# A decode kernel of two attention and two gated blocks: the 78 matmuls of constants on TensorE are left out

## The chip, the cores and the metric

The kernel runs on one core of one Trainium2 chip. The core has five engines with a queue of instructions each: TensorE (PE; its weight loads are listed apart as PEld), VectorE (DVE), ScalarE (ACT), GpSimd (POOL) and SyncE (SP), which here only issues DMAs. The metric is the device time in microseconds of one execution, as the median of several runs. A profile of one further execution gives the time of each instruction. A tile in SBUF lies on 128 partitions; matmuls write to PSUM, whose eight banks of 128 x 512 float32 are all in use here.

## The reference

Four tokens (a batch of 4, one position each) of width 512 go twice through the same attention block and the same gated block, with residuals and a layer norm without parameters ahead of each:

```python
def _A_ref(x, k_cache, v_cache, wq, wo):          # 32 query heads, 8 key/value heads, 4096 positions, head size 128
    q = (x @ wq).reshape(B, Sq, Hq, Dh).transpose(0, 2, 1, 3)
    k = jnp.repeat(k_cache, 4, axis=1)
    v = jnp.repeat(v_cache, 4, axis=1)
    p = softmax(einsum("bhqd,bhkd->bhqk", q, k) * Dh ** -0.5)
    o = einsum("bhqk,bhkd->bhqd", p, v)
    return o.transpose(0, 2, 1, 3).reshape(B, Sq, Hq * Dh) @ wo

def _B_ref(x, w_gate, w_up, w_down):              # width 1792 inside
    return (sigmoid(x @ w_gate) * (x @ w_up)) @ w_down

x = x + A(layernorm(x)); x = x + B(layernorm(x))
x = x + A(layernorm(x)); x = x + B(layernorm(x))
```

The caches are in bfloat16. One head of one batch element has 4096 x 128 keys and as many values, 1 MB each, and there are 32 of each kind. Both layers read the same caches.

## The kernel before

**Units and pairs.** A unit is one key/value head of one batch element in one layer: 64 units, taken as 32 pairs of heads in the order of the table `ORDER` (lines 22 to 55). Pairs of the second layer start as soon as their batch element has gone through its gated block, while other elements are still in the first layer.

**Memory.** SBUF has 12 slots of 1 MB (tile `slot`) and four more that hold `wq` at first (tile `wq`). Each slot holds the keys or the values of one unit. Some are kept for the second layer (`RET`), the others are loaded again. Loads are issued by SP in the order of the table `LOADS`; `pump` (line 523) issues as many as there are free slots. A load into a slot waits for the last reader of what was there before, and since SP's queue is in order, later loads wait behind it. `wo` and the gated block's weights have places of their own and come in the same order.

**Steps.** The main loop (line 1822) has 33 steps. In step k the scores and the softmax of pair k are worked out and the values of pair k-1 are applied. By tile and line: the keys are transposed in place by DVE in blocks of 32 x 32 (L1165, 2.2 us a slot); TensorE multiplies them with the queries into `S_ps` (`scores`, L1181); DVE takes the largest (`smax`, L1218 to L1224), TensorE spreads it (`spread_max`, L1241), DVE negates it (L1254), ACT takes the exponential and its sum (L1266), TensorE sums over partitions (`sums`, L1289) and DVE inverts (`inverse`, L1299); TensorE transposes the probabilities into `PT` (`ptrans`, L1311), ACT and DVE copy them to `pT` in 16 parts (L1345 and L1339); TensorE applies the values (`pv`, L1415) into `O_ps`, DVE divides (L1506), TensorE applies `wo` (L1567, or L1537 and L1550 in another form) and DVE adds to the token (L1588).

**Passes.** When all pairs of a batch element in the first layer are done, a pass of 23 pieces takes it through the layer norm, the gated block, the next layer norm and the queries of the second layer: sums for the norm on TensorE (L753, L815) with a reciprocal root by Newton steps on DVE (L781, L797), the up and gate projections (L974), the turning and the down projection (L1017, L1088, L1110), the query projection (L1035), its turning (L1066) and spreading (L879), and POOL's blocks (`q_blocks`, L904), on which the scores of that element's first pair wait. There are four passes, for four elements, at about 89 to 110, 143 to 163, 194 to 212 and 249 to 267 us.

**What sets the order.** Nothing is scheduled by a planner: each engine runs its instructions in the order in which the program records them. The order is written out in tables. Each step has nine places, 0 to 8, at which `do_steps(k, w)` is called (line 1666), and the tables say at which place of which step a piece of a pass, a turn of `wo`, or the first half of the next scores stands. Waits are worked out from what is read and written under names: `S.group` makes an instruction wait for the last writer and the readers since, and `prune` drops the waits that others already imply.

**The fills.** The table `FILL` (lines 150 to 155) says at which places constants are multiplied, and how many times. `fill(n)` (line 1197) records n matmuls on TensorE of the identity with the identity twice side by side, 128 x 256, into columns 256 to 511 of the bank `MS`, which nothing reads. It is recorded as reading the identity and as writing the names `MS` and `MSs`, so that the first matmul of a group waits for the readers of the maximum (DVE L1254) and of the sums (DVE L1299), and the next writer of either name waits for the group on TensorE itself. `do_steps` calls it ahead of the other pieces of its place; `tail_fill` calls it in the tail (key 33).

**The tail.** After the last pair's scores the values of that pair come in quarters (L1442). The last token's `wo` (L1776), its mean by weights summed earlier (L1798), the last gated block for all four tokens (L921, L2020), and the output follow.

Of the kernel before, what the change touches and what calls it, by code (L numbers as in the profile page):

```python
# [146 lines left out]
)  # L147


FILL = {  # L150
# [4 lines left out]
}  # L155


WSUM = (
# [153 lines left out]
def bass_interleave_layers__gqa_block_cached__glu_gated_glu__decode_kernel(  # L312
# [884 lines left out]
    def fill(n):  # L1197
        wide_id = ident_bf[:, :].unsqueeze(1).broadcast_to([P, 2, P])
        fns = [
            lambda e: e.matmul(  # L1200
                MS[:, 2 * P:4 * P].rearrange("p (i m) -> p i m", i=2), lhsT=ident_bf[:, :], rhs=wide_id,
                start=True, stop=True,
            )
        ] * n
        S.group("pe", fns, reads=IDENT, writes=["MS", "MSs"])

    def tail_fill(i):
        if FILL.get((NP + 1, i)):
            fill(FILL[NP + 1, i])

# [384 lines left out]
    def finish():  # L1595
        while undone:
            undone.pop()()
# [68 lines left out]
    def do_steps(g, w):  # L1666
        finish()
        if FILL.get((g, w)):
            fill(FILL[g, w])
        for m in wo_steps.pop((g, w), ()):  # L1670
# [459 lines left out]
```

## Time and profile before

| what | before |
|---|---|
| median of 3 runs | 303.74 us (303.08 to 305.57) |
| profiled execution, its own time | 306.06 us |
| its span, first to last instruction | 304.3 us |
| mean granted TensorE clock | 0.826 |
| TensorE, weight loads, DVE, ACT, POOL busy | 220.8, 154.8, 208.0, 133.0, 26.4 us |
| read from HBM | 115.61 MB, 380 GB/s over the span |
| matmuls of L1200 | 78, 14.9 us busy |

How to read the page and the views: PE's busy time counts a matmul from its start to its modelled end, so overlapping ones are counted once. A row of the windows view gives a stretch of the span, its length, the busy us of PE, PEld, DVE, ACT and POOL with the number of instructions, the granted clock (1.00 is full speed), the busy share of the 16 DMA engines, and GB/s. A row of the timeline gives the start, the length from the first to the last of a run of like instructions, the engine, the line and the operation with output and input, and in brackets the idle time ahead and what ended it. A row of the chain of waits gives start, length and what was on the chain. "issue" stands where the profile shows nothing that was waited for.

### The profile page before, as it was taken

Reading aid. Unit: us, or ns where it says so; the run is one execution under the profiler, and the core shown is the slowest. Engines: PE = TensorE matmul, PEld = TensorE weight load, DVE = VectorE, ACT = ScalarE, POOL = GpSimd, SP = SyncE. Lnnn points to the kernel's source line nnn. Section 1 sums busy time; section 2 is a strip of 40 time slices with the busy share of each in tenths; the row PEclk is TensorE's granted clock in tenths of the full one; section 3 lists DMA queues with packets and bytes.
Section 4 is the critical chain, followed back from the end, with each engine's and each line's share of the span. In section 5 each row is a group of like instructions: output and inputs, shape, how many; then the busy total and the mean of one; then the engine's idle time right before and its main releaser. Section 6 shows DMA issues by size and latency. Waiting matters only on the chain.

```text
span 304.3 us, 11550 instructions
## 1 busy us (share of the span) xinstructions
PE 220.8 (73%) x5030; PEld 154.8 (51%) x5030; DVE 208.0 (68%) x599; ACT 133.0 (44%) x531; POOL 26.4 (9%) x108
## 2 busy tenths in 40 slices
PE   0373577367479877977897876987686968958896
PEld 0331135234355565566565554754455855646695
DVE  4745899496567457986853987776796578648724
ACT  1031344152514334755371784635483552536510
POOL 0000000000000001100001100001000000012200
PEclk9995559695957967579997776999879799995979
DMA  7999999999999979999999999999999998999800
GB/s 284 419 403 415 412 415 421 415 418 419 417 421 402 386 277 424 426 418 418 403 420 421 415 422 415 423 415 423 416 423 415 378 417 323 392 400 423 328 11 3
DMA packets 19166, 116.35 MB, mean 382 GB/s; under 512 B 1960, under 2 KB 1964, under 8 KB 6444
## 3 DMA queue, kind: packets, MB, share of 16 engines
q1 hardware_dynamic: 19116, 115.62, 93.3%
q8 instruction: 39, 0.64, 0.8%
q14 instruction: 11, 0.09, 0.1%
HBM read 115.61 MB, written 0.00 MB: 380 GB/s over the span
## 4 chain that ended last, share of the span: by engine, by line
DMA 38%; PE 31%; DVE 19%; ACT 4%; issue 3%; SPq 3%; POOL 0%; DVEq 0%
DMA slot<-in_A_v_cache_dram 14%; DMA wo<-in_A_wo_dram 13%; DMA slot<-in_A_k_cache_dram 11%; PE O_ps L1415 8%; DVE slot L1165 7%; PE S_ps L1181 5%; PE O_ps L1567 3%; DVE pT L1339 2%; ACT pT L1345 2%; PE MS L1200 2%; SPq L551 2%; DVE small L1218 1%; DVE wq L1165 1%; PE M_ps L974 1%; PE M_ps L1035 1%
## 5 line engine op out<-in xcount | busy, mean ns | idle before, releaser
L1165 DVE STREAM_TRANSPOSE slot<-slot 128x2048 f32<-128x2048 f32 (+1 forms) x57 | 100.5, 1771 | 8.0 <-DMA slot<-in_A_k_cache_dram 8.0
L1345 ACT ACTIVATE pT<-PT 32x64 bf16<-32x64 f32 x404 | 86.9, 215 | 33.0 <-PE PT L1311 27.9
L1415 PE MATMUL O_ps<-pT,slot 128*128 128x32 bf16 (+2 forms) x1920 | 64.1, 188 | 15.7 <-DMA slot<-in_A_v_cache_dram 6.7
L1415 PEld LDWEIGHTS O_ps<-pT,slot 128*128 128x128 bf16 x1920 | 58.6, 101 | 20.9 <-DMA slot<-in_A_v_cache_dram 8.1
L1181 PE MATMUL S_ps<-slot,qz 128*32 128x256 bf16 x992 | 48.8, 336 | 14.6 <-DVE slot L1165 10.6
L1181 PEld LDWEIGHTS S_ps<-slot,qz 128*32 128x32 bf16 x992 | 25.4, 109 | 28.8 <-DVE slot L1165 13.6
L1266 ACT ACTIVATE pe<-S_ps,small 128x256 bf16<-128x256 f32 x32 | 15.2, 474 | 54.0 <-DVE small L1254 53.8
L1280 POOL TENSOR_TENSOR small<-small 128x1 f32<-128x1 f32 x64 | 12.5, 195 | 219.3 <-ACT pe L1266 216.8
L647 ACT ACTIVATE wo<-M_ps 128x512 bf16<-128x512 f32 x14 | 8.4, 596 | 45.7 <-PE M_ps L637 45.6
L637 PE MATMUL M_ps<-wo,row 64*128 64x512 bf16 x56 | 12.8, 541 | 13.6 <-DMA wo<-in_A_wo_dram 10.7
L1339 DVE CAST pT<-PT 32x64 bf16<-32x64 f32 x92 | 20.3, 221 | 3.2 <-PE PT L1311 1.8
L1567 PE MATMUL O_ps<-oT,wo 128*128 128x32 bf16 x608 | 20.6, 188 | 2.0 <-DVE oT L1506 1.5
L1567 PEld LDWEIGHTS O_ps<-oT,wo 128*128 128x128 bf16 x608 | 19.2, 101 | 3.3 <-DVE oT L1506 2.1
L1218 DVE TENSOR_REDUCE small<-S_ps 128x1 f32<-128x256 f32 x32 | 13.3, 415 | 7.5 <-PE S_ps L1181 7.3
L652 DVE CAST wo<-M_ps 128x512 bf16<-128x512 f32 x14 | 9.6, 686 | 10.3 <-PE M_ps L637 10.1
L904 POOL TENSOR_TENSOR qz<-qc,norm 128x128 bf16<-128x128 bf16 x32 | 12.6, 401 | 44.4 <-ACT qc L890 44.4
L1200 PE MATMUL MS<-ident_bf 128*128 128x256 bf16 x78 | 14.9, 324 | 2.0 <-DVE rden L1299 1.5
L1311 PE MATMUL PT<-ident_bf,pe 128*128 128x128 bf16 x64 | 10.3, 252 | 4.8 <-ACT pe L1266 4.1
L1506 DVE TENSOR_TENSOR oT<-O_ps,rden 128x8 bf16<-128x8 f32 x31 | 4.9, 159 | 11.7 <-PE O_ps L1415 8.4
L1254 DVE CUSTOM_DVE_ANT_0 row_max<-MS,small 128x16 bf16<-128x16 f32 x32 | 7.0, 217 | 7.6 <-PE MS L1241 7.6
L637 PEld LDWEIGHTS M_ps<-wo,row 64*128 64x128 bf16 x56 | 2.1, 102 | 18.0 <-issue 11.1
L1241 PE MATMUL MS<-row_max,mask_f 128*128 128x16 bf16 x64 | 6.6, 176 | 6.1 <-DVE row_max L1224 5.5
(142 smaller groups left out, 227.1 us busy)
## 6 DMA issues: line engine op xcount, KB each, us to landing
slot<-in_A_v_cache_dram SPq DMA_DIRECT2D x48, 1024.0 KB, 10.6
slot<-in_A_k_cache_dram SPq DMA_DIRECT2D x43, 1024.0 KB, 11.3
wq<-in_A_wq_dram SPq DMA_DIRECT2D x4, 1024.0 KB, 7.7
wo<-in_A_wo_dram SPq DMA_DIRECT2D x8, 512.0 KB, 16.0
wq<-in_A_k_cache_dram SPq DMA_DIRECT2D x2, 1024.0 KB, 11.8
wq<-in_A_v_cache_dram SPq DMA_DIRECT2D x2, 1024.0 KB, 15.8
slot<-in_A_v_cache_dram SPq DMA_DIRECT2D x8, 256.0 KB, 18.4
wg<-in_B_w_gate_dram SPq DMA_DIRECT2D x2, 896.0 KB, 15.8
```

What stands on the lines that cost most here:

```text
L637: (lambda h, i, rows: lambda e: e.matmul(ps[h][:, :], lhsT=spread_w[i][rows, :], rhs=wo_sb[rows, c + i, :], start=(i == 0), stop=(i == 1), ...
L904: lambda e: e.tensor_tensor(qz_sb[z][:, :, 0:4 * REP].rearrange("p i (a r) -> p i a r", r=REP), qc_sb[:, b, u:u + 2, :, :].rearrange("p u ...
L1165: dve(lambda e: e.transpose(kf, kf), writes=[f"s{st}"])
L1181: (lambda t, b2, e_, w0, s: lambda e: e.matmul(S_ps[p][32 * s:32 * s + 8 * REP, 0:2 * P], lhsT=qzf[:, w0:w0 + 8 * REP], rhs=ktv[:, :, s, : ...
L1200: lambda e: e.matmul(MS[:, 2 * P:4 * P].rearrange("p (i m) -> p i m", i=2), lhsT=ident_bf[:, :], rhs=wide_id, start=True, stop=True,)
L1218: lambda e: e.tensor_reduce(m, S_ps[p][:, 0:2 * P], AX.X, ALU.max),
L1266: lambda e: e.activation(to, frm, ACTF.Exp, bias=nm_sb[p], scale=exp_scale, accum_out=sm_sb[p][0],),
L1280: (lambda n: lambda e: e.tensor_tensor(sm_sb[p][n + 1], sm_sb[p][n], top(sm_sb[p][n]), ALU.subtract))(n),
L1339: (lambda dst, frm: lambda e: e.tensor_copy(dst, frm))(dst, frm),
L1345: (lambda dst, frm: lambda e: e.activation(dst, frm, ACTF.Copy))(dst, frm),
L1415: (lambda x, c, j: lambda e: e.matmul(O_ps[p][:, ul * OW:ul * OW + PV_WIDE[g]].rearrange("p (w n) -> p w n", n=REP), lhsT=vv[:, x * JG + c ...
L1567: (lambda c, r: lambda e: e.matmul(wide_out(O_ps[p], OWO + c, nb), lhsT=wo_sb[:, u * REP + r, bass.ds(2 * P * (c // 2) + c % 2, P, step=2) ...
```

## The change

The table of fills becomes empty. `fill`, `tail_fill` and their calls stay in the text and record nothing. No other table, tile or instruction is touched.

```diff
-FILL = {
-    (3, 1): 2, (3, 7): 8, (5, 2): 8, (5, 8): 6, (6, 4): 6, (7, 1): 1,
-    (8, 3): 1, (9, 1): 2, (11, 6): 4, (12, 1): 3, (12, 7): 3, (15, 1): 1,
-    (16, 8): 3, (18, 1): 5, (18, 8): 3, (25, 0): 6, (25, 8): 8, (26, 7): 4,
-    (31, 0): 1, (33, 1): 3,
-}
+FILL = {}
```

The key of an entry is a step and a place (33 stands for the tail), its value the number of matmuls.

## The prediction

> **What bounds the kernel now.** I read the page first (busy time, clock, queues, the group of the constant matmuls), then the chain of waits, then the busy time in windows, and last the timeline around each group of constant matmuls (I call them fills, after their table).
>
> ```profile
> span 304.3 us, 11550 instructions
> PE 220.8 (73%) x5030; PEld 154.8 (51%) x5030; DVE 208.0 (68%) x599; ACT 133.0 (44%) x531; POOL 26.4 (9%) x108
> ...
> PEclk9995559695957967579997776999879799995979
> ...
> q8 instruction: 39, 0.64, 0.8%
> ...
> L1200 PE MATMUL MS<-ident_bf 128*128 128x256 bf16 x78 | 14.9, 324 | 2.0 <-DVE rden L1299 1.5
> ```
>
> No engine is busy throughout. The last row is all that is removed: 14.9 us of TensorE's 220.8. If all of it were on the path, 303.7 would fall to 289; if none were, only the clock row could move.
>
> The windows view gives busy us, the granted clock and, last, GB/s.
>
> ```profile
> 104.00:108.00 4.00, 3.31 (x67) 1.61 (x68) 1.95 (x9) 0.69 (x1) 0.00 (x0) 1.00 0.87 328
> 108.00:112.00 4.00, 3.02 (x67) 1.81 (x63) 2.43 (x12) 1.90 (x9) 0.76 (x2) 0.69 0.69 240
> ...
> 116.00:120.00 4.00, 2.38 (x69) 1.72 (x57) 3.45 (x7) 2.34 (x11) 0.15 (x1) 0.93 1.02 428
> ...
> 232.00:236.00 4.00, 1.83 (x48) 1.20 (x48) 3.90 (x12) 2.52 (x11) 0.74 (x3) 0.97 1.02 422
> ```
>
> From 116 to 236 (the last two rows are the first and last of 30) the queue stays full: compute may come a little early or late there without moving the end. Between 104 and 112 it is not full, so there a late free slot costs time. After 247 it is the engines alone that are on the chain:
>
> ```profile
> 97.56 0.66 PE MS L1200 x6
> ...
> 246.97 2.31 DVE slot L1165
> ...
> 269.59 2.51 issue
> ```
>
> The transpose at 246.97 starts when its tile lands; no DMA stands on the chain behind it. So three stretches count: 97 to 112, 247 to 287, and the tail. Fills before 97 (18) and between 113 and 236 (25) lie in stretches where transfers set the pace; I price them at nothing, and the cover is the full queue, its loads landing 10.6 us after issue (the row below), so that a free slot may come several us late. Without that cover each would be worth at most its own 0.19 us (14.9 over 78).
>
> ```profile
> slot<-in_A_v_cache_dram SPq DMA_DIRECT2D x48, 1024.0 KB, 10.6
> ```
>
> **The change part by part.** The built program's order shows 78 matmuls fewer on TensorE and nothing moved elsewhere; some waits on TensorE's own semaphore go with them, two DVE waits gain DVE's own semaphore, long set, and SP's queue is unchanged.
>
> *First, 97 to 112 us.*
>
> ```profile
> 97.40 0.81 PE L1200 MATMUL MS<-ident_bf 128*128 128x256 bf16 x6
> 98.15 0.66 PE L1181 MATMUL S_ps<-slot,qz 128*32 128x256 bf16 x16
> 101.86 0.55 PEld L1110 LDWEIGHTS M_ps<-sel,row 128*128 128x128 f32 x4 [0.29 <-ACT row L1103]
> 104.83 1.71 PE L1035 MATMUL M_ps<-wq,xc_bf 128*1 128x512 bf16 x24
> 107.16 0.17 PEld L1066 LDWEIGHTS M_ps<-ident_bf,row 128*128 128x128 bf16 x4 [1.12 <-ACT row L1049]
> ```
>
> The six fills at 97.40 push the scores of L1181 back: a gain of 0.66 (the chain's row). The six at 101 end where L1110 waits for ScalarE anyway: nothing. The single one at 112.1 I put at its own 0.2. So 0.86 may be gained. Against it stands the clock, next.
>
> *The clock.* Cut into steps of 3.41 us the granted clock is 1.00 or 0.50 in every step:
>
> ```profile
> 65.12:68.53 3.41, 1.86 (x66) 1.76 (x66) 3.33 (x6) 1.40 (x5) 0.00 (x0) 1.00 1.01 418
> ...
> 99.26:102.67 3.41, 2.98 (x56) 2.00 (x54) 1.36 (x8) 2.23 (x9) 0.39 (x2) 1.00 1.01 418
> ...
> 160.70:164.11 3.41, 1.34 (x51) 1.00 (x50) 1.02 (x3) 0.28 (x1) 0.76 (x2) 1.00 1.01 418
> 164.11:167.52 3.41, 3.24 (x76) 2.20 (x68) 1.73 (x7) 1.28 (x6) 0.57 (x3) 0.50 1.01 418
> ...
> 286.99:290.40 3.41, 2.72 (x64) 2.04 (x61) 2.13 (x12) 1.80 (x7) 1.15 (x7) 1.00 0.31 115
> ```
>
> The step at 160.70, in which TensorE is busy 1.34 of 3.41 (0.39) at full clock, is followed by one at half. Of the 50 steps at full clock from 24 us on, all nine under 0.6 were followed by half clock (the busiest of them is the first row, 0.55), and five of the sixteen from 0.6 to 0.8 (the busiest is the last row, 0.80). Back to full clock it takes a step busy about 0.9. So what the fills buy is the *next* step's clock. In the step at 99.26 there are six fills, about 0.8 us (as at 97.40) of its 2.98 busy (0.87); without them 0.64, the undecided zone. Half clock from 102.7 on would stretch L1035's 24 matmuls of 1.71 us by some 1.2 (an estimate: eight like ones of 448 columns cost 0.35 more, below, three times that and 512/448), of which 0.4 or so is covered by the wait for ScalarE at 107.16 (1.12 with the row): 0.85 lost. Half a chance of it: 0.4. Term: -0.86 + 0.4 = **-0.4**, bounds -0.9 and 0.
>
> The Trainium skill, page "TensorE: Matmul & The Clock Gate", section "Why this matters for your kernels", says the clock is lost only by idle gaps over some 3 us. By that rule the removal, which opens no such gap, would cost no clock; in the trace, though, TensorE never stood 3.4 us in the step at 160.70, which has 51 matmuls, and the clock fell. That result of the rule is the first rival.
>
> *Second, 247 to 257 us.*
>
> ```profile
> 246.03:249.44 3.41, 2.21 (x51) 1.67 (x43) 2.55 (x4) 2.88 (x14) 0.74 (x3) 1.00 1.01 423
> ...
> 246.03:249.44 3.41, 1.03 (x8) 0.70 (x8) 1.00 1.01 423
> ...
> 249.38 0.30 PEld L753 LDWEIGHTS M_ps<-xT,small 128*128 128x128 f32 x2 [1.12 <-DVE xT L1588]
> 250.22 0.57 PE L974 MATMUL M_ps<-wu,xc_bf 128*1 128x448 bf16 x8 [0.46 <-DVE xc_bf L766]
> 250.63 0.64 PE L1181 MATMUL S_ps<-slot,qz 128*32 128x256 bf16 x16
> 252.99 0.96 PE L974 MATMUL M_ps<-wg,xc_bf 128*1 128x448 bf16 x16
> ...
> 92.08 0.92 PE L974 MATMUL M_ps<-wu,xc_bf 128*1 128x448 bf16 x8
> ...
> 88.43 1.04 PE L1181 MATMUL S_ps<-slot,qz 128*32 128x256 bf16 x16
> ```
>
> The first two rows are the same step, whole and fills alone: 2.21 busy, 1.03 of it fills. Without them 1.18 of 3.41 = 0.35, under every step that kept its clock. The eight fills themselves sit under DVE's transpose (L753 waits for xT behind it), so leaving them out gains nothing. But the next step runs at half clock, and by the last two rows (taken at half clock) a group of eight L974 costs 0.92 for 0.57 and the scores 1.04 for 0.64. The normalisation and up projection have two groups of eight (0.35 each), one of scores (0.40), and the gate's sixteen (0.70): 1.8. The step at 249.44 would then be busy about 0.75 (it stands idle until 250.22), too little to come back, so the second step is at half clock as well. Some 0.3 us of the gate's lateness is hidden by the DVE transposes. Term **+1.5**; bounds 0 (the clock holds) and +2.7 (it stays down over the q rows at 260 too, 32 matmuls of L1035, an estimated 1.6 by the same scaling, 0.4 of it covered).
>
> *Third, the code pages.* Fetches of instructions come on q8: 39 of 16 KB, one for some 258 of TensorE's 10,060 instructions.
>
> ```profile
> 272.10 0.25 PEld L1415 LDWEIGHTS O_ps<-pT,slot 128*128 128x128 bf16 x7 [2.83 <-issue]
> ...
> q8 instruction: 1, 0.02, 5.9%
> ...
> q8 instruction: 1, 0.02, 5.5%
> ...
> 264.69:272.10 7.41, 4.00 (x136) 3.35 (x131) 3.71 (x19) 3.19 (x13) 1.15 (x4) 1.00 0.96 380
> ...
> 263.50:267.75 4.25, 3.58 (x134) 3.30 (x134) 3.10 (x14) 1.62 (x8) 1.15 (x4) 1.00 0.93 362
> 267.75:275.10 7.35, 4.61 (x133) 3.53 (x125) 2.68 (x15) 2.66 (x11) 0.74 (x3) 0.88 1.01 416
> ```
>
> TensorE stands 2.74 us until 272.10 in the middle of a group of L1415 with no release shown. The first q8 row is that of the window 269.80:270.80: a page came just then, 1.3 us before work went on. I read it as: TensorE ran out of code. If a page is called when the one before it begins, which is my assumption, the call was 256 instructions earlier, at 264.69 (first window row), and the fetch, queued behind data, took 7.4 us from call to use. The next page, called at 272.10, came in the window 275.70:276.80 (second q8 row): 4.6 us, and 5.9 with the same 1.3. Seventy-four of the fills lie ahead, 148 instructions, so the page edges move to what now stands at 263.50, 267.75 and 275.10. Between these lie 4.25 us and, less the standing 2.74, 4.61 us of work; both are shorter than a fetch. With fetches of 6.6 (the mean of the two) and 5.9 us TensorE stands 2.35 and 1.3, together 3.65 for 2.74: **+0.9**. Bounds: -2.7 (the standing vanishes) and +3.2 (both fetches near 7.4).
>
> The Trainium skill, page "Runtime: NRT & Kernel Launch", section "Instruction fetch mechanics", calls the cost of crossing such a block mostly hidden. By that alone this term would be 0 and the sum 0.9 less; the row at 272.10 speaks against it.
>
> *Fourth, the tail.*
>
> ```profile
> 287.33 0.28 PE L1200 MATMUL MS<-ident_bf 128*128 128x256 bf16 x1
> 287.55 0.61 PE L1537 MATMUL O_ps<-wo,oT 128*2 128x256 bf16 x16
> 296.10 0.56 PEld L1776 LDWEIGHTS S_ps<-oT,wo 128*128 128x128 bf16 x16 [0.21 <-DVE oT L1732]
> ```
>
> The one at 287.33 holds L1537 back by 0.2; the three at 295.7 end under DVE's oT: nothing. The ten at 241 and 259 end under a landing and under DVE, too. Term **-0.2**, bounds -0.5 and 0.
>
> Sum: -0.4 + 1.5 + 0.9 - 0.2 = **+1.8**. The profiled execution took 306.06 (span 304.3 and 1.8 around it); the median of the runs shown is 303.74. On the median: **305.5**.
>
> **Rivals.** *The fills are plain cost.* If the clock does not follow a step's busy time, only the gains stay: 0.86 and 0.2, 302.7. For it: the six at 97.56 stand on the chain. Against: nine of nine idle steps lost the clock. Its sharper form ends beyond 1% on the fast side: the page edges move off the dense stretch, TensorE no longer stands at 269.4, and 2.74 more go, 299.9. It decides if a page's call has over 5.9 us of work ahead of it at 264 to 275; my windows of 4.25 and 4.61 speak against.
>
> *Half clock spreads.* The q rows at 104 and at 260 run at half clock too: 0.45 (the full 0.85 for the half counted) and 1.2 above the forecast, and 0.5 for the per-pair work between: 307.6; with late pages at their bound, 309.9. For it: 78 fills went into steps that are near the edge. Against: those passes are dense themselves, 0.87 and more in most steps.
>
> *Transfers hide it all.* The queue is full over most of the span, and the loss after 247 is met by the idle stretch at 269.4: 303.7. Against: after 246.97 no DMA is on the chain.
>
> **How the numbers follow.** Forecast (304.0 to 307.0 around 305.5) 0.45; fills plain cost 0.20 and with the page gone 0.05; half clock spreads 0.22; hidden 0.08. One per cent, 3.0 us, is about what a measurement of this kernel tells from no change. Faster by more: only the 0.05. Slower by more (over 306.8): 0.22 and the forecast's upper edge, together 0.30. The rest, 0.65, within. The range 302.0 to 309.0 leaves out the vanished page and the worst of the spreading; the sum of all upper bounds (+5.9) ends at 309.6, that of all lower ones (-4.1) at 299.6.
>
> **What would show it.** In the changed profile: no rows of the fills; the clock row lower on the whole, at half clock in the steps from 249; L974 at 0.9 us for eight there; the scores at 97 earlier by 0.6; two standings of TensorE with "issue" between 266 and 276 in place of one; the same GB/s from 116 to 236. Wrong I would be if the clock is kept at 249, if TensorE's standing near 270 is gone, or if GB/s falls between 116 and 236, which would mean that slots come free too late there.

## The result, and the profile after

| | before, same chip | after |
|---|---|---|
| median of 4 runs | 304.65 us (303.08 to 307.87) | 308.26 us (307.27 to 308.90) |
| ratio, 95% interval | 1 | 1.0112 (1.0072 to 1.0152) |
| profiled execution, its span | 306.06, 304.3 us | 308.54, 305.9 us |
| mean granted TensorE clock | 0.826 | 0.794 |

The kernel is slower by 1.1%, 3.4 us of 304.65 (2.2 to 4.6 by the interval). The forecast was +1.8: the right direction, half the size. The median of 308.26 us lies within the stated range of 302.0 to 309.0, but above the forecast's own stretch (304.0 to 307.0), and the change is just over the 1% within which the prediction put 0.65 of its chances. A ratio leaves out the executions over 1.5% above the fastest of their kernel; in the experiments below these are 22 of 80 of the kernel before and 5 of 110 of the others (three far longer ones, named at the end, are left out as well), so the table there gives the ratio of the medians of all executions as well, which is up to 0.6% lower.

From the page of the kernel after, with the GB/s row:

```profile
span 305.9 us, 11386 instructions
PE 218.4 (71%) x4952; PEld 152.4 (50%) x4952; DVE 208.5 (68%) x599; ACT 132.6 (43%) x531; POOL 26.2 (9%) x108
...
PEclk9999999575756899555598558799956996997977
...
GB/s 283 421 402 419 407 417 421 414 420 418 418 419 402 391 256 417 422 416 416 357 376 421 403 422 419 423 413 423 419 417 412 392 416 305 336 391 423 398 62 3
```

The first thing to see is TensorE's busy time. Fills of 14.9 us are gone, and it fell by 2.4 only (220.8 to 218.4): what stayed got longer. The clock row goes with it: the 17th to the 20th slice (7.65 us each, 122 to 153 us) read 5555 where before read 5799, the 23rd and 24th (168 to 184) 55 for 77. In the GB/s row the 15th slice (107 to 115 us) has 256 for 277, the 20th and 21st (145 to 161) 357 and 376 for 403 and 420. The first slices of the clock rows can't be compared: the trace of the kernel after has no record of the clock before 43.1 us, and 1.00 stands where there is none (sixteen matmuls of scores at 29 us take 1.04 us in both traces, the time that the prediction shows at half clock). So the mean of 0.794 above is too high, if anything.

The windows view (busy us of PE, PEld, DVE, ACT, POOL; clock, DMA share, GB/s) at the first pass and at the second, kernel after:

```profile
104.00:108.00 4.00, 3.93 (x38) 1.14 (x38) 1.40 (x8) 0.69 (x1) 0.00 (x0) 0.57 0.87 328
108.00:112.00 4.00, 3.03 (x98) 2.34 (x98) 2.89 (x11) 1.89 (x9) 0.76 (x2) 1.00 0.48 182
144.00:148.00 4.00, 3.11 (x41) 1.79 (x34) 2.88 (x8) 1.63 (x8) 0.00 (x0) 0.50 0.93 367
148.00:152.00 4.00, 4.00 (x85) 2.27 (x86) 3.58 (x11) 1.62 (x4) 0.39 (x2) 0.50 0.98 354
152.00:156.00 4.00, 3.61 (x104) 2.71 (x100) 2.52 (x11) 3.14 (x14) 0.00 (x0) 0.96 0.92 360
156.00:160.00 4.00, 3.73 (x72) 2.21 (x76) 2.84 (x18) 2.38 (x11) 0.38 (x2) 1.00 1.01 377
```

The same four windows of the second pass in the kernel before:

```profile
144.00:148.00 4.00, 3.38 (x84) 2.24 (x84) 3.35 (x19) 1.57 (x6) 0.39 (x2) 1.00 1.02 406
148.00:152.00 4.00, 2.62 (x71) 1.86 (x64) 3.60 (x7) 1.81 (x8) 0.00 (x0) 1.00 1.01 416
152.00:156.00 4.00, 3.52 (x103) 3.03 (x102) 1.78 (x12) 2.48 (x10) 0.20 (x1) 1.00 1.02 414
156.00:160.00 4.00, 3.93 (x92) 2.08 (x88) 2.57 (x14) 3.27 (x13) 0.20 (x1) 1.00 1.00 418
```

From 104 to 108 the clock is 0.57 where it was 1.00 and TensorE is busy 3.93 us with 38 matmuls, where it did 67 in 3.31; behind it, 108 to 112, the DMA engines move 182 GB/s where it was 240. From 144 to 152 the clock is 0.50 where it was 1.00, and from 144 to 160 the transfers, at 406 to 418 before, run at 354 to 377. So transfer is lost behind two passes that are slow by their clock.

The matmuls of the query projection in the first pass, in the timeline of before and then of after:

```profile
103.98 0.60 PE L1035 MATMUL M_ps<-wq,xc_bf 128*1 128x512 bf16 x8 [0.46 <-DVE xc_bf L766]
```

```profile
103.96 0.60 PE L1030 MATMUL M_ps<-wq,xc_bf 128*1 128x512 bf16 x8 [0.46 <-DVE xc_bf L761]
105.00 2.97 PE L1030 MATMUL M_ps<-wq,xc_bf 128*1 128x512 bf16 x24
```

(Lines behind the table are 5 lower in the kernel after: L1035 is L1030 there.) They start at the same time, and the 24 that took 1.71 us take 2.97. This is the stretch that the prediction's first term priced, 1.26 us where it estimated 1.2.

The steps of 3.41 us around it, kernel after:

```profile
101.12:104.54 3.42, 2.25 (x47) 1.73 (x47) 0.73 (x5) 0.66 (x3) 0.38 (x2) 1.00 1.01 390
104.54:107.95 3.41, 3.34 (x32) 0.98 (x29) 1.24 (x7) 0.69 (x1) 0.00 (x0) 0.50 0.83 329
```

The step at 101.12 is busy 0.66 (2.25 of 3.42) and is followed by half clock, as steps of 0.6 to 0.8 sometimes are. With the fills the step at the same place of the work was at 0.87.

What is lost there arrives at the last pass as a late landing. The transpose of keys ahead of that pass starts when its tile lands, in before and then in after:

```profile
246.97 2.31 DVE L1165 STREAM_TRANSPOSE slot<-slot 128x2048 f32<-128x2048 f32 x1 [0.71 <-DMA slot<-in_A_k_cache_dram]
```

```profile
249.19 2.31 DVE L1160 STREAM_TRANSPOSE slot<-slot 128x2048 f32<-128x2048 f32 x1 [0.83 <-DMA slot<-in_A_k_cache_dram]
```

It is 2.2 us late. The two spans differ by 1.6, so all of this pair's loss has arisen by then: from here to the end the kernel after takes 56.7 us and the kernel before 57.3.

The late part of the chain of waits (start, length, what), one row of before and then the kernel after:

```profile
262.54 0.69 ACT row L1049
```

```profile
243.11 2.20 issue
...
249.42 2.00 issue
...
252.22 0.60 PE M_ps L748 x2
253.27 0.92 PE M_ps L969 x8
...
267.20 0.69 ACT row L1044
```

The last pass starts 2.8 us late (L748 at 252.22; L753 stood at 249.38). The late transpose ends at 251.50; the rest, some 0.5, is the standing of TensorE that ends at 251.41, behind which the token's last sum comes. The standing of 2.20 us at 243 is over before the tile lands. The pass itself starts at half clock (eight of L969 at 0.92) and ends 4.7 us late (the queries' copy by ACT at 267.20, for 262.54). A part of this comes back: in before TensorE's standing of 2.51 us at 269.59 lies behind the pass, and it is gone here, while another of 1.34 has come. At its end the kernel after is only 1.6 us late.

### The profile page after: what moved, and what is told of

It reads as the page before. It is cut to its first block, busy times and chain, and to the rows that moved or that the text cites. A ratio compares the mean times of both kernels' runs of the same rounds, so it can differ in the third digit from the quotient of the medians.

```text
span 305.9 us, 11386 instructions
## 1 busy us (share of the span) xinstructions
PE 218.4 (71%) x4952; PEld 152.4 (50%) x4952; DVE 208.5 (68%) x599; ACT 132.6 (43%) x531; POOL 26.2 (9%) x108
## 4 chain that ended last, share of the span: by engine, by line
DMA 33%; PE 32%; DVE 18%; ACT 8%; issue 4%; SPq 3%; POOL 0%; DVEq 0%; ACTq 0%
DMA wo<-in_A_wo_dram 13%; DMA slot<-in_A_v_cache_dram 12%; PE O_ps L1410 10%; DVE slot L1160 10%; DMA slot<-in_A_k_cache_dram 8%; ACT pT L1340 6%; PE S_ps L1176 5%; PE O_ps L1562 3%; PE M_ps L969 2%; SPq L546 2%; DVE pT L1334 1%; PE M_ps L1030 1%; ACT pe L1261 1%; PE M_ps L632 1%; DVE small L1213 1%
## 5 line engine op out<-in xcount | busy, mean ns | idle before, releaser
L1410 PE MATMUL O_ps<-pT,slot 128*128 128x32 bf16 (+2 forms) x1920 | 65.4, 190 | 13.4 <-DMA slot<-in_A_v_cache_dram 6.3
L1410 PEld LDWEIGHTS O_ps<-pT,slot 128*128 128x128 bf16 x1920 | 60.2, 102 | 18.4 <-DMA slot<-in_A_v_cache_dram 7.2
L1176 PE MATMUL S_ps<-slot,qz 128*32 128x256 bf16 x992 | 51.1, 348 | 14.5 <-DVE slot L1160 10.6
L1176 PEld LDWEIGHTS S_ps<-slot,qz 128*32 128x32 bf16 x992 | 26.1, 113 | 29.4 <-DVE slot L1160 14.1
L1236 PEld LDWEIGHTS MS<-row_max,mask_f 128*128 128x128 bf16 x64 | 4.3, 107 | 15.5 <-DVE row_max L1219 13.3
L1030 PE MATMUL M_ps<-wq,xc_bf 128*1 128x512 bf16 x128 | 10.4, 422 | 1.5 <-DVE xc_bf L761 1.3
```

What stands on the lines that cost most here:

```text
L1030: (lambda k, st: lambda e: e.matmul(M_ps[h][32 * st:32 * st + 1, :], lhsT=xc_bf[:, k, 0:1], rhs=wv[:, k, h, :, st, :], start=(k == 0), sto ...
L1176: (lambda t, b2, e_, w0, s: lambda e: e.matmul(S_ps[p][32 * s:32 * s + 8 * REP, 0:2 * P], lhsT=qzf[:, w0:w0 + 8 * REP], rhs=ktv[:, :, s, : ...
L1410: (lambda x, c, j: lambda e: e.matmul(O_ps[p][:, ul * OW:ul * OW + PV_WIDE[g]].rearrange("p (w n) -> p w n", n=REP), lhsT=vv[:, x * JG + c ...
```

## The experiments

Three readings had to be told apart: the forecast's own (clock at the last pass, code pages in the last stretch), the rival "half clock spreads" (the clock at the passes from the first on), and the rival "plain cost". Two numbers are given for each kernel beside its ratio, both from its one profiled execution. Most kernels ran 12 times, "none again" and "late kept" 6 times, the kernel after and "all short, again" 4 times. *q* is the time from the start of the first to that of the last query-projection matmul in the first pass: 2.2 at full clock, 3.4 to 3.8 at half. *Lost transfer* is the sum over windows of 4 us of 4·(1 - GB/s / 418), from 100 to 120 and from 140 to 164 together, that is behind the first two passes.

### What the shape of the fills does

```diff
 def fill(n):  # all 78 stay, with 8 columns each in place of 256
-    MS[:, 2 * P:4 * P].rearrange("p (i m) -> p i m", i=2), lhsT=ident_bf[:, :], rhs=wide_id,
+    MS[:, 2 * P:2 * P + 8], lhsT=ident_bf[:, :], rhs=ident_bf[:, 0:8],
```

> All 78 constant matmuls stay in place, with their waits, but each streams 8 columns instead of 256: TensorE's instruction count and so the edges of its code pages are those of the kernel before, while its array time for constants falls from 14.9 us to about 2. Clock alone. If clock and code pages both count (my account): slower than before by 0.3 to 0.9% (1 to 3 us), without the two standings of 2 us at 243 and 249 that the changed kernel has, and with one of about 2.7 us near 269 as in the kernel before. If the clock alone makes the loss: the full 1.1%. If code pages alone do: within 0.2% of the kernel before.

> All 78 constants in place with 8 columns each, once more, since the first profile of it ran throughout at a slower clock than any other. If the short ones, with their weight loads, still hold part of the clock: query projection of the first pass under 3 us and lost transfer from 100 to 164 between those of the kernels with and without constants (3 and 5 us), 0.3 to 0.8% over the kernel before. If not: as the changed kernel, 3.4 to 3.8 us, 5 to 6 us and 1.0 to 1.5%.

The first gave 1.0048 (1.0011 to 1.0085) against before, the second 1.0134 (1.0051 to 1.0217). The intervals overlap, and together they say slower, by something between half a per cent and the whole loss. The profile of the first cannot be used (its execution took 479.74 us, below). That of the second reads as with no fills: q 3.8, lost transfer 5.4, and the step ahead of the lost clock (busy 0.73), then the matmuls themselves:

```profile
99.07:102.49 3.42, 2.48 (x61) 1.80 (x54) 1.01 (x7) 2.27 (x10) 0.39 (x2) 1.00 1.02 422
```

```profile
105.44 2.97 PE L1035 MATMUL M_ps<-wq,xc_bf 128*1 128x512 bf16 x24
```

Here every instruction, wait and page edge of before is in its place, and only the time that the fills keep TensorE busy is gone. So it is that time that pays; whether short fills keep some of the clock is left open by the two ratios.

### Page edges moved alone

```diff
+    # ahead of the main loop, before 12 us: the page edges of the kernel after, with all fills kept
+    S.group("pe", [lambda e: e.matmul(MS[:, 2 * P:2 * P + 8], lhsT=ident_bf[:, :],
+        rhs=ident_bf[:, 0:8], start=True, stop=True)] * 49, reads=IDENT)
```

> The kernel before with all its constants, and 49 matmuls of 8 columns (98 instructions) more in the wait for the first weights, before 12 us. Late in the kernel the change has 158 instructions fewer, and 98 more move the edges of 256-instruction pages to the same places of the program (158 + 98 = 256). Code pages alone. If pages count: TensorE stands some 2 us twice near 243 to 250, in the L1562/L1567 groups of those two places, and no longer near 269; time 0.3 to 0.8% over the kernel before. If the standings have another cause: they stay where the kernel before has them (269), and time within 0.2%.

Measured 1.0028 (0.9995 to 1.0061); q 2.2, lost transfer 3.8. And the reverse, the kernel after with 79 such matmuls, which puts the edges back to where before had them:

> The changed kernel (no constants) with 79 matmuls of 8 columns (158 instructions) in the wait for the first weights, before 12 us, so that the late page edges fall on the same places of the program as in the kernel before. If clock and code pages both count: as e1_short, 0.3 to 0.9% over the kernel before, standing near 269 to 274 and none of 2 us at 243 and 249. If the clock alone: 1.1%. If pages alone: within 0.2%.

Measured 1.0112 (1.0071 to 1.0154), the ratio of the kernel after ("none again", in another round, has 1.0149); q 3.8, lost transfer 5.2. The standings did move. In the timeline of the first, then of the second:

```profile
249.38 0.22 PE L1567 MATMUL O_ps<-oT,wo 128*128 128x32 bf16 x2 [1.77 <-issue]
```

```profile
272.80 0.25 PEld L1410 LDWEIGHTS O_ps<-pT,slot 128*128 128x128 bf16 x7 [1.18 <-issue]
```

With the moved edges TensorE stands ahead of the last pass, as in the kernel after, but only once for long (1.77 us) where two such standings were expected; with the edges put back it stands in the group of `pv` again, where before had its 2.74, and also for 1.46 us at 245.02, where before did not. With TensorE's instructions in each trace numbered from 0, every such standing of 1 us or more, in all usable profiles, ends at a number that leaves 193 or 194 when divided by 256. So the places follow the count, which goes with the reading that TensorE waits for code pages there; whether it stands at such a place, and how long, differs. But their sum changes the time by 0.28% at the most likely, with an interval that reaches zero, and putting them back gains nothing.

### The eight at the last pass alone

```diff
-fill(FILL[g, w])
+fill(FILL[g, w], 4 if (g, w) == (25, 8) else P)  # 2 x 4 columns for these eight
 # (not shown: in `fill` the second argument cuts the columns)
```

> Only the eight constants at about 247.5 (step 25, place 8) are shortened to 8 columns each, in place; the other 70 are whole. Same instruction count and page edges as before. By the forecast's second term: half clock in the two steps from 249, L974's eights at 0.92 us there, slower by 1.5 us (0.5%). If the clock holds or the delay is absorbed later: within 0.2%.

Measured 0.9992 (0.9961 to 1.0024). The windows and the timeline of its last pass, and last the row of L1017 in before:

```profile
244.00:248.00 4.00, 1.99 (x60) 1.57 (x48) 2.75 (x6) 3.31 (x15) 0.74 (x3) 0.85 1.03 416
248.00:252.00 4.00, 3.54 (x46) 1.74 (x46) 2.61 (x11) 0.91 (x5) 0.00 (x0) 0.52 0.86 311
252.00:256.00 4.00, 3.59 (x63) 1.89 (x60) 2.70 (x7) 0.95 (x2) 0.00 (x0) 0.58 0.91 352
```

```profile
247.68 0.39 PE L753 MATMUL M_ps<-xT,small 128*128 128x4 f32 x2 [1.66 <-DVE xT L1589]
248.53 0.92 PE L974 MATMUL M_ps<-wu,xc_bf 128*1 128x448 bf16 x8 [0.46 <-DVE xc_bf L766]
253.07 1.66 PE L974 MATMUL M_ps<-wg,xc_bf 128*1 128x448 bf16 x16
256.16 0.52 PE L1017 MATMUL M_ps<-ident_bf,row 128*128 128x2 bf16 x8 [0.57 <-DVE row L1002]
```

```profile
255.69 0.52 PE L1017 MATMUL M_ps<-ident_bf,row 128*128 128x2 bf16 x8
```

The second term's mechanism is there in each of its parts: half clock from 248 to 255, eight of L974 at 0.92, and from L753 to L1017 it takes 8.5 us where before took 6.3. (In this one profile the clock is 0.85 at most from 43 us on, where the others have 1.00; its time is nonetheless among the shorter ones of this kernel.) Yet the time is that of before. A part of the reason is in the same trace, at the place where before stood for 2.74 us:

```profile
271.30 0.35 PE L1416 MATMUL O_ps<-pT,slot 128*128 128x32 bf16 x8 [1.31 <-issue]
```

TensorE stands there for 1.31, so 1.4 of the 2.2 us are taken back: the forecast added the late pass and this standing, but the one uses up the other. The remaining 0.8 is about the upper end of what the twelve executions allow (+0.7).

The whole eight do not always hold the clock either. In the trace with moved edges, which has all its fills, it is lost at 250.14:

```profile
246.73:250.14 3.41, 1.64 (x41) 1.47 (x40) 2.48 (x2) 3.03 (x15) 0.62 (x3) 1.00 1.01 413
250.14:253.55 3.41, 2.95 (x35) 1.81 (x32) 1.73 (x5) 0.41 (x2) 0.00 (x0) 0.50 0.70 291
```

```profile
249.45 1.24 PE L1200 MATMUL MS<-ident_bf 128*128 128x256 bf16 x8
```

There TensorE's standing of 1.77 us had pushed the fills to 249.45, so that a part of them fell into the next step. The steps of 3.41 us also begin at another place of the work (246.73, for 246.03 in before), but that this alone would lose the clock is not shown: cut at 246.73, the stretch of before is busy 2.19 us, nearly as in its own step (2.21, or 0.65, a share at which the next step is undecided).

### Which fills

The table of fills was cut in several ways; nothing else differs. Steps and places as in the table.

```diff
 # none again:      FILL = {}
 # early kept:      the 44 of steps 3 to 12 stay, the 34 of steps 15 to 33 go
 # late kept:       the other way round
 # no twelve:       only (5, 8): 6 and (6, 4): 6 go, the fills at 97 and 101 us
 # only twenty:     only (5, 2): 8, (5, 8): 6 and (6, 4): 6 stay
 # no thirteen:     only (8, 3), (9, 1), (11, 6), (12, 1), (12, 7) go, 13 fills from 120 to 151 us
```

> The changed kernel once more, on the chip and beside the runs of the kernel before that the next two share. Account now: half clock spreads, and the time is lost where the transfer queue runs dry in the first two passes (before 164 us): GB/s under 400 in several stretches of 4 us between 100 and 164, 2 us more of lost transfer there than in the kernel before; slower by 0.8 to 1.2%. If chance in the clock's phase made the first measurement: 0.2 to 0.5%.

> The 44 constants of steps 3 to 12 (until 151 us) stay, the 34 of steps 15 to 33 go. If the loss arises in the first two passes: within 0.3% of the kernel before. If it arises from 240 us on, as the forecast's second and third terms say: 0.6 to 1.1% slower.

> The other half: the 44 constants of steps 3 to 12 go, the 34 of steps 15 to 33 stay. If the loss arises in the first two passes: 0.7 to 1.2% slower, with 1.5 us or more of lost transfer between 140 and 164. If from 240 us on: within 0.3%.

> Of the 78 only the twelve at 97 and 101 us (steps 5 and 6) are left out, those whose first six the forecast counted as a gain of 0.66 us with half a chance of 0.85 lost. Account now (half clock in the first pass): the query projection of that pass (32 matmuls of L1035, first to last start) takes 3.4 to 3.8 us in place of 2.2, the pass about 1 us longer than the 16.1 to 17.5 of the kernels that have all early constants, 1 us more transfer lost from 100 to 120, time 0.2 to 0.5% over the kernel before. If the twelve are plain cost: pass 1 shorter by 0.6 us, time 0.2% under it.

> Only the 20 constants at 89.9, 97.4 and 101.0 us stay. If they keep the clock of the first pass: its query projection at 2.2 to 2.4 us, the pass 16 to 17.5, transfer lost from 100 to 120 about 2 to 3 us as in the kernel before, and half of the loss of the changed kernel goes: 0.4 to 0.8% over the kernel before. If the first pass does not matter: 1.1 to 1.5% as without any.

> The thirteen constants of steps 8 to 12 (120 to 151 us), ahead of the second pass and at its start, are left out, the other 65 stay. If they keep the clock ahead of the second pass: half clock over most of 120 to 150, the pass 18 to 19.5 us in place of 17.5 or starting 1 us later, 1 us more transfer lost from 140 to 164, time 0.2 to 0.5% over the kernel before. If the full queue hides them, as the forecast said: pass and lost transfer as before, time within 0.2%.

Measured, with the runs above beside them, in the order of lost transfer. The last column is the start of the transpose ahead of the last pass, shown above for before and after:

| kernel | ratio to before (95%) | medians of all | q, us | lost transfer, us | last transpose, us |
|---|---|---|---|---|---|
| only the eight at (25, 8) short | 0.9992 (0.9961 to 1.0024) | 0.998 | 2.3 | 2.0 | 245.3 |
| early kept | 1.0066 (1.0027 to 1.0106) | 1.004 | 2.2 | 2.3 | 245.8 |
| before | 1 | 1 | 2.2 | 3.1 | 247.0 |
| no thirteen | 0.9995 (0.9955 to 1.0035) | 0.997 | 2.2 | 3.4 | 246.9 |
| all, edges moved | 1.0028 (0.9995 to 1.0061) | 1.000 | 2.2 | 3.8 | 247.1 |
| only twenty | 1.0097 (1.0053 to 1.0141) | 1.007 | 2.2 | 4.2 | 248.6 |
| no twelve | 1.0078 (1.0039 to 1.0118) | 1.006 | 3.7 | 4.8 | 248.1 |
| late kept | 1.0160 (1.0093 to 1.0226) | 1.010 | 3.8 | 5.0 | 249.4 |
| none, edges put back | 1.0112 (1.0071 to 1.0154) | 1.007 | 3.8 | 5.2 | 248.4 |
| all short, again | 1.0134 (1.0051 to 1.0217) | 1.011 | 3.8 | 5.4 | 248.7 |
| after | 1.0112 (1.0072 to 1.0152) | 1.012 | 3.4 | 5.5 | 249.2 |
| none again | 1.0149 (1.0095 to 1.0203) | 1.011 | 3.8 | 5.7 | 249.6 |

The last column bears the reading out: all seven kernels that lost 4.2 us of transfer or more reach the last transpose at 248.1 to 249.6 us, the other five at 245.3 to 247.1. From there to the end the twelve profiles take 56.2 to 59.2 us, in no order that goes with the fills.

*The twelve.* They lie in the first pass of the forecast, and leaving them out alone costs 0.8% (0.6% by the medians of all). The clock at the query projection parts the kernels without exception: all five profiles in which the twelve are gone have q at 3.4 or more, and so has the one in which all fills are short; the six with the twelve at their length have 2.2 or 2.3. The steps of "no twelve", and its matmuls:

```profile
94.40:97.81 3.41, 2.52 (x65) 1.95 (x61) 2.75 (x3) 3.00 (x13) 0.00 (x0) 1.00 1.08 404
97.81:101.22 3.41, 2.12 (x30) 0.90 (x30) 1.22 (x7) 1.92 (x8) 0.36 (x2) 0.50 1.01 418
101.22:104.64 3.42, 2.84 (x42) 2.72 (x46) 0.65 (x5) 0.06 (x1) 0.02 (x1) 0.50 0.90 371
104.64:108.05 3.41, 3.34 (x30) 0.98 (x26) 1.31 (x8) 0.49 (x1) 0.00 (x0) 0.50 0.93 329
```

```profile
104.50 1.02 PE L1049 MATMUL M_ps<-wq,xc_bf 128*1 128x512 bf16 x8 [0.46 <-DVE xc_bf L780]
105.97 2.59 PE L1049 MATMUL M_ps<-wq,xc_bf 128*1 128x512 bf16 x24
```

The step at 94.40, in which the six at 97 would begin, is busy 0.74 and the clock goes; with the twelve away nothing brings it back before 108. In the window from 108 to 112 this kernel's transfers fall to 98 GB/s (before: 240).

```profile
108.00:112.00 4.00, 3.02 (x90) 2.10 (x93) 2.34 (x9) 1.67 (x8) 0.75 (x2) 0.99 0.35 98
```

*The early ones.* Keeping 44 early fills takes 0.8% off the loss (1.0149 to 1.0066), with full clock from 92 to 108 and from 140 to 160 us and 403 to 424 GB/s in the latter. Late fills alone take nothing off (1.0160). So with the early ones gone the late ones are worth nothing that these intervals show; with the early ones kept, the 34 late ones are worth 0.66%, or 0.35% by the medians of all, which is hardly clear of the noise. By the middle values the two parts do not add up; the spread of the runs leaves that undecided. Eight of them, those at (25, 8), are worth nothing. Which of the other 26 matter is left open; the profile of "early kept" has the span of before, 304.3 us, and so does not show it.

*The thirteen.* They lie where the queue of transfers is full, and cost nothing alone. Without them the second pass does start at half clock, its first eight of L974 (here L985) taking 0.96 us for 0.58; yet the pass takes 17.6 us from its first up projection to the copy of its queries, for 17.5 in before, and 0.3 us of transfer is lost from 140 to 164, for 0.2:

```profile
145.51 0.96 PE L985 MATMUL M_ps<-wu,xc_bf 128*1 128x448 bf16 x8
```

"Only twenty", which has the clock at 104 again, keeps most of the loss. Its second pass starts at half clock too (here L973), but 0.4 us later, the half clock is there from 136 us on (in "no thirteen" from 144), and the pass takes 18.3 us with 1.0 us of transfer lost:

```profile
145.88 0.95 PE L973 MATMUL M_ps<-wu,xc_bf 128*1 128x448 bf16 x8
```

So half clock at the second pass costs nothing that shows in the one profile, and comes with a loss in the kernels in which other fills are gone too. How much lateness the queue covers is left open. That no single group carries the loss is what the rival "half clock spreads" said.

## Why the prediction was half right

*Direction and mechanism.* The rule that the forecast read from the 50 steps at full clock of one trace, that a step with TensorE busy under 0.6 loses the next step's clock and one of 0.6 to 0.8 may, held in the runs. In the eleven other profiles that have a record of the clock (counted from 24 us or from where the record begins, and with 0.85 as full clock in the one that has no 1.00), 97 of 105 such steps under 0.6 were followed by half clock (all 76 under 0.55), 54 of 145 between 0.6 and 0.8, and 8 of 220 above. The steps at 101.12 (0.66), 94.40 (0.74) and 246.73 (0.48) are among them. The advice of the Trainium skill (page "TensorE: Matmul & The Clock Gate", section "Why this matters for your kernels"), to leave no idle gap over some 3 us, was not enough here: none of these three steps, with 41 to 65 matmuls each, holds such a gap. The rival "plain cost", 302.7, falls with it. That the sum came out on the right side was in part luck: what the forecast put before 247 us was a gain of 0.4, and what it put behind, the other three terms, a loss of 2.2; in the profiled pair 2.2 us are lost by 247 and 0.6 is gained behind it.

*First term, -0.4: this is the step that failed.* It gave half clock at the query projection half a chance, set it against 0.86 us gained from the path, and came out as a gain. The half clock comes in every profile without the twelve. Its price on the matmuls was sized rightly (1.26 measured, 1.2 forecast, in the kernel after, whose first eight still ran at full clock; q is up to 1.6 longer elsewhere); but it is not covered by ScalarE's wait, and it spreads over the pass: from its first up projection to the copy of its queries the first pass takes 17.9 to 18.7 us in these profiles and 16.1 to 17.5 in the others. Behind the pass some 1 us of transfer is lost (4.1 without the twelve from 100 to 120, 2.9 in before). "No twelve" measures the term but for the single fill at 112: +0.8%, 2.4 us (1.2 to 3.6; 1.9 by the medians of all), where -0.4 was forecast. The difference, 2.8, is more than the whole miss of 1.6, since the second term came to nothing. With the measured values the sum is 2.4 + 0 + 0.85 - 0.2 = 3.05, for 3.4 measured; since groups of fills need not add up (early and late, above), that closeness proves little.

*Second term, +1.5.* Right in each part of its mechanism, and worth 0 (-1.2 to +0.7 us): "The eight at the last pass alone". It counted the delay of the pass as if it reached the end; in the trace 1.4 of 2.2 us went into a shorter standing of TensorE behind the pass. The rival "transfers hide it all" had said just this of the idle stretch at 269.4. Whether the eight hold the clock in every execution stays open.

*Third term, +0.9.* That TensorE's standings follow the count of instructions is borne out by the two kernels that move the edges and nothing else. Of the two that were forecast one came, at its place and in its size (L1289 stood at 275.41 in before; 1.34 us measured, 1.3 forecast):

```profile
278.19 0.20 PE L1284 MATMUL MS<-head_b,small 128*128 128x8 bf16 x2 [1.34 <-issue]
```

The other, of 2.35 us at what stood at 267.75, did not. Two of 2.20 and 2.00 us came at 243 and 249 instead; the forecast had looked only at edges inside the last dense stretch, and by the chain these are, all but some 0.5 us, covered by the late landing. The price was +0.28% (-0.15 to +1.9 us) when the edges were moved alone, and 0 when they were put back (the two equal ratios leave some 0.6% either way): consistent with 0.9 and with nothing. The Trainium skill's "mostly hidden" (page "Runtime: NRT & Kernel Launch", section "Instruction fetch mechanics") is thus not contradicted as to the end, though TensorE's rows show the crossings.

*Cover from 113 to 236.* I named GB/s falling between 116 and 236 as what would make me wrong, and it fell, to 367 and 354 from 144 to 152. The full queue covers the thirteen fills there, as forecast, when they are all that is missing, half clock at the start of the second pass included. It does not cover a second pass that starts late (146.6 for 145.1) and runs at half clock. That the first pass makes the second late is likely from the order of the work, and not shown apart.

*Tail, -0.2.* Not measured apart; the profiles do not contradict it.

*The rivals.* "Half clock spreads" was nearer the truth than the forecast, in size (307.6) and in kind: it is the passes that lose the clock, not the last one alone. It had named the query rows at 104, but priced them on the chain only, without the transfers that a late pass leaves out. Its largest part, 1.2 for the query rows of the last pass, did not come: in the kernel after they run at full clock (the first eight, at 264.54, take 0.60 us). "Transfers hide it all" is refuted for the first two passes, and partly right about the last.

No variant is faster than before beyond its interval; two with fewer or shorter fills ("no thirteen", "only the eight short") are as fast.

## What to carry to other kernels

Work that only fills a wait is to be judged by the step of the clock after it: on the path it costs its own few tenths, and what it buys is the speed of the dense matmuls that come next, so it matters ahead of dense work that something else waits for, here a pass on which slots and then transfers depend. Where a term hangs on a step that is only just busy enough, and on whether a fill falls into this step or the next, one profiled execution shows one case: look for a second, or give the term both values. A delay and a standing behind it are not to be added before it is clear that the one does not use up the other. And a kernel that is bound by transfers loses its time where the queue runs short: count the missing GB/s there before pricing the engines' chain at the end.

## What was unexpected of the hardware

The 256-instruction rule of TensorE's standings was not looked for (those of 1 us or more end at a number that leaves 193 or 194 modulo 256); they run up to 2.74 us, in the one execution of each kernel that was profiled.

In one profile, that of "only the eight short", the granted clock is 0.85 or 0.50 in place of 1.00 or 0.50, and eight of L974 take 0.61 us at 0.85 for 0.57.

One execution of the kernel with short fills took 479.74 us, and it was the profiled one; one of the kernel before took 503.0, and one of "only twenty" 333.15. In the profile of the first TensorE's busy time is nearly doubled, while DVE's and ACT's stay:

```profile
span 478.0 us, 11550 instructions
PE 436.7 (91%) x5030; PEld 287.5 (60%) x5030; DVE 210.5 (44%) x599; ACT 133.8 (28%) x531; POOL 26.3 (5%) x108
```

That would go with TensorE at a lower speed from end to end: the 24 matmuls of the first pass's query projection take 4.92 us there, for 2.97 at half clock. The trace holds no record of the clock for this execution, and the 1.0 listed for it says no more than that; the cause is open. Beside these, executions of one and the same kernel before ran from 302.2 to 310.5 us. In each of the three rounds the shorter ones have the higher mean clock (correlation -0.58 to -0.76, 80 executions in all, with a mean that counts stretches without a record as 1.00); that the phase of the clock's steps is behind this spread is a guess that no run here tests.
